# Attention backward: one block of E goes by way of GpSimd into the tile that a DMA transposes, and E lies in a ring of eleven steps

## The chip, the cores and the metric

The kernel runs on one core of a Trainium2 chip. The metric is the time of one execution on the device in microseconds (us); lower is better. The core has the matmul engine (PE; PEld is its loading of weights), VectorE (DVE), ScalarE (ACT), GpSimd (POOL) and SyncE (SP, which here only issues DMA transfers), and 16 DMA engines. PE, DVE, ACT, POOL and SP each run their own instructions in order and wait for one another by semaphores.

## The reference

Forward and gradients of `x + attention(LN(x)) * silu(MLP(LN(x)))`, for 2048 rows, width 512, 32 heads of 16 and a hidden width of 1792, all in bfloat16. Cut to the part that the change touches:

```python
qkv = (x @ wqkv).reshape(B, S, 3, H, Dh).transpose(2, 0, 3, 1, 4)
q, k, v = qkv[0], qkv[1], qkv[2]
scores = jnp.einsum("bhqd,bhkd->bhqk", q, k) * (Dh ** -0.5)
p = softmax(scores)
o = jnp.einsum("bhqk,bhkd->bhqd", p, v)
...
out, vjp = jax.vjp(f, A_x, A_wqkv, A_wo, B_w1, B_b1, B_w2, B_b2)
grads = vjp(grad_out)
```

With E = exp(scores - bound), D = dO V^T and G = D * E, the gradients of a head need E and G twice: with the keys on the partitions, as they are computed, and with the queries on the partitions, that is transposed.

## The kernel before

The attention loop (`attention_core`) takes two heads at a time (16 pairs) and 512 queries at a time (4 chunks): 64 blocks. Within a block it goes through the 2048 keys in 16 steps of 128 keys (`kb` 0 to 15), 1024 steps in all. The order of the work on every engine is written out by hand: the loop over `g` emits the parts of a step, and parts of earlier steps, in a fixed order, and each engine keeps it.

In step `g`, for both heads (`hj`), PE makes `s` (the scores of step g+1, L1115) and `d` (L1137) in PSUM; ACT writes the exponential of `s` into the tile `ets` (L1124), 8 blocks of 128 keys x 128 queries, numbered b = 2 * (query block) + head; DVE multiplies `d` by E into `gts` (L1153), one tile for two steps; PE adds up `X` (L1248, L1251, L1255), whose operands are E and G as they lie, and one step later transposes blocks of E through PSUM into `tT` (L1208, L1212). ACT, and DVE for a few blocks, copies these to the tile `ek` (L1224, L1231). `ek` holds 7 of the 8 blocks of E; the first block is left out of it in odd chunks of four steps, the last in even ones.

Two things are transposed by DMA, issued from SP (`emit_dmat`). All of G: after every second step one DMA transposes the 16 blocks of a `gts` tile into half a `gk` tile (L1170). And the one block of E that `ek` leaves out: a DMA transposes the four blocks of four steps, or eight blocks of two adjacent chunks at once, from `ets` into the tile `ekd` (L1180, L1184, L1186). It is issued in the steps with `kb % 8` of 4 and 6, so that a pair of chunks takes one issue or two, by where it lies in the ring. For this `ets` lies in three slots of four steps, `[128, 3, 4, 2, 4, 128]`: within a slot a block's four steps are neighbours. A slot's step is overwritten twelve steps later.

Twenty steps behind (`ZOFF`), `emit_z` (L1350) multiplies the transposed G (four steps of PE, one for each query block) and then the transposed E (four more) by small tiles `W` into `Z`, four matmuls a step; DVE adds `Z` to `acc` (L1362, L1364). GpSimd prepares `W` and the outputs of a block in two halves (`emit_fin`, L1311 to L1329), stores finished sums (`ob`, L1368 and L1371), and issues the loads of the next pair of heads, each behind a small copy `tick` (L1420), which waits for the step's products and so paces them. Tiles are reused in rings: `gts` 4, `gk` 6, `ekd` 3, `ek` 7.

Of the kernel before, what the change touches and what calls it, by code (L numbers as in the profile page):

```python
# [8 lines left out]
bf16 = mybir.dt.bfloat16  # L9
f32 = mybir.dt.float32  # L10
ACT = mybir.ActivationFunctionType
ALU = mybir.AluOpType
# [1038 lines left out]
def attention_core(ctx, ctx_r, tc, k, grads, Oall, dQall, dKVT_out, ident_f32, ident_bf, npairs=16, nqc=4):  # L1051
    nc = tc.nc
# [51 lines left out]
    def emit_s(g, hj):  # L1104
        a = a_unit(g)
        if a is None:
            return
        j, kb = a
        op = op_of(j)
        qc = blocks[j][1]  # L1110
        r = 32 * hj
        if hj == 0:
            cur["s"] = ps_s.tile([128, 2, 512], f32, name="s")
        s = cur["s"]
        nc.tensor.matmul(s[:, hj, :], lhsT=op["KVT"][r:r + 32, kb * 128:(kb + 1) * 128], rhs=op["QDT"][r:r + 32, qc * 512:(qc + 1) * 512],  # L1115
                         start=True, stop=True, tile_position=(r, 0))
        st_et[g] = ets[:, g // 4 % 3]

    def emit_exp(g):

        a = a_unit(g)
        if a is None:
            return
        nc.scalar.activation(out=st_et[g][:, :, :, a[1] % 4, :].rearrange("k b h q -> k h b q"),  # L1124
                             in_=cur["s"][:].rearrange("k h (b q) -> k h b q", b=4), func=ACT.Exp)

    def emit_d(g, hj):
# [13 lines left out]
    def emit_mult(g):  # L1141
        a = a_unit(g)
        if a is None:
            emit_xs(g - 1)
            emit_acc(g + ZOFF)
            return
        kb = a[1]
        if kb % 2 == 0:
            cur["gts"] = gtp.tile([128, 2, 2, 512], bf16, name="gts")
        gts = cur["gts"]  # L1150
        st_gt[g] = gts
        for hj in range(2):
            nc.vector.tensor_tensor(out=gts[:, kb % 2, hj, :].rearrange("k (b q) -> k b q", b=4),  # L1153
                                    in0=st_d.pop((g, hj))[:].rearrange("k (b q) -> k b q", b=4),
                                    in1=st_et[g][:, :, hj, kb % 4, :], op=ALU.mult)
            if hj == 0:
                emit_xs(g - 1)
                emit_acc(g + ZOFF)

    def emit_dmat(g):  # L1160
        a = a_unit(g)
        if a is None:
            return
        j, kb = a
        kc = kb // 4
        if kb % 4 == 1:
            blk[j]["Gk"][kc] = gbp.tile([128, 4, 2, 4, 128], bf16, name="gk")
        if kb % 2 == 1:
            gk = blk[j]["Gk"][kc][:, kb % 4 - 1:kb % 4 + 1]
            nc.sync.dma_start_transpose(out=gk.rearrange("q r h b k -> q (r h b) k"), in_=st_gt[g][:].rearrange("k a h q -> k (a h q)"))  # L1170


        sl = g // 4 % 3
        if kb % 8 == 4:
            ek = ekd.tile([128, 2, 4, 128], bf16, name="ekd")
            blk[j]["Ek"][(kc - 1, 3)] = ek[:, 0]
            blk[j]["Ek"][(kc, 3)] = ek[:, 1]
            blk[j]["ekd"] = ek
            if sl == 0:
                nc.sync.dma_start_transpose(out=ek[:, 0], in_=ets[:, 2, 3, 1].rearrange("k a q -> k (a q)"))  # L1180
        if kb % 8 == 6:
            ek = blk[j].pop("ekd")
            if sl == 0:
                nc.sync.dma_start_transpose(out=ek[:, 1], in_=ets[:, sl, 0, 0].rearrange("k a q -> k (a q)"))  # L1184
            else:
                nc.sync.dma_start_transpose(out=ek[:].rearrange("q c a k -> q (c a) k"),  # L1186
                                            in_=ets[:].rearrange("k s b h a q -> k (s b h) (a q)")[:, 8 * sl - 1:8 * sl + 1]
                                            .rearrange("k x q -> k (x q)"))

    OLDER = {4: (0, 0), 6: (0, 1), 7: (0, 2), 8: (5, 0), 12: (5, 1), 13: (5, 2)}  # L1190

# [6 lines left out]
    def emit_T(g):  # L1198
        a = a_unit(g)
        if a is None:  # L1200
            return
        kk = a[1] % 4
        et = st_et[g]
        t = ps_t.tile([128, 512], f32, name="tT")
        tb = t[:].bitcast(bf16).rearrange("q (i k) -> q i k", k=128)
        for i in range(cut(g), 7):
            b = i + a[1] // 4 % 2
            nc.tensor.transpose(tb[:, i - cut(g), :], et[:, b // 2, b % 2, kk, :], ident_bf[:])  # L1208
        if older(g):
            kk2, i = older(g)  # L1210
            b = i + kk2 // 4 % 2
            nc.tensor.transpose(tb[:, 7, :], st_et[g // 16 * 16 + kk2][:, b // 2, b % 2, kk2 % 4, :], ident_bf[:])  # L1212
# [20 lines left out]
    def emit_x(g, part):  # L1233
        a = a_unit(g)
        if a is None:
            return
        j, kb = a
        if part == "e" and kb == 0:
            blk[j]["X"] = ps_x.tile([128, 512], f32, name="X", tag="X")
        X = blk[j]["X"]  # L1240
        NATt = op_of(j)["NAT"]
        et = st_et[g]
        for c in range(4):
            half, hj = c // 2, c % 2
            r = 32 * c
            ev = et[:, half::2, hj, kb % 4, :]
            if part == "e":
                nc.tensor.matmul(X[r:r + 32, 0:256], lhsT=NATt[:, kb, hj, 1:33], rhs=ev,  # L1248
                                 start=(kb == 0), stop=False, skip_group_check=True, tile_position=(0, r))
            elif part == "l":  # L1250
                nc.tensor.matmul(X[r:r + 32, 256:512], lhsT=Lc[:], rhs=ev,  # L1251
                                 start=False, stop=False, skip_group_check=True, tile_position=(0, r))
            else:
                gv = st_gt[g][:, kb % 2, hj, :].rearrange("k (b q) -> k b q", b=4)[:, half::2, :]
                nc.tensor.matmul(X[r:r + 17, 256:512], lhsT=NATt[:, kb, hj, 0:17], rhs=gv,  # L1255
                                 start=False, stop=(kb == 15), skip_group_check=True, tile_position=(0, r))

# [74 lines left out]
    def emit_z(g):  # L1332
        u = z_unit(g)
        if u is None:
            return
        j, kp, qb, part = u
        if part == 0 and qb == 0:
            blk[j]["Z"] = ps_z.tile([128, 512], f32, name="Z", tag="z")
        Z = blk[j]["Z"]
        for par in range(2):  # L1340
            kc = 2 * kp + par
            for hj in range(2):
                r = 64 * par + 32 * hj
# [6 lines left out]
                nc.tensor.matmul(Z[r:r + 32, :], lhsT=WT[j % 2][1 - part][:, qb, hj, :], rhs=mv,  # L1350
                                 start=(part == 0 and qb == 0), stop=(part == 1 and qb == 3), tile_position=(0, r))

    def emit_acc(g):
        u = z_unit(g)
        if u is None or u[2] != 3 or u[3] != 1:
            return
        j, kp = u[0], u[1]
        p, qc = blocks[j]
        Z = blk[j]["Z"]
        av = acc[:, kp, :]  # L1360
        if qc == 0:
            nc.vector.tensor_copy(out=av, in_=Z[:])  # L1362
        else:
            nc.vector.tensor_tensor(out=av, in0=Z[:], in1=av, op=ALU.add)  # L1364
        if qc == nqc - 1:
            ob = (outp.tile([128, 512], bf16, name="ob") if kp == 0 or j < NB - 1 else
                  xsp.tile([128, 512], bf16, name="ob", tag="xs"))
            nc.gpsimd.tensor_copy(out=ob[:], in_=av)  # L1368
# [11 lines left out]
    for g in range(NSTEP - ZOFF):  # L1380
# [36 lines left out]
        for it in [x for x in late if x[0] <= g]:  # L1417
            late.remove(it)

            nc.gpsimd.tensor_copy(out=tick[:], in_=st_gt[g][0:1, kb % 2, 1, 510:512])  # L1420
            it[1]()
        if g >= NSTEP:
            grads.tail_mid(g - NSTEP)
# [120 lines left out]
```

## Time and profile before

| | us |
|---|---|
| median of three runs | 2192.32 |
| lowest and highest | 2185.16 and 2199.84 |
| the profiled execution | 2194.69 |
| its span | 2193.0 |

The attention loop fills the span from about 220 to 1870 us; what lies ahead of it (norms, projections, the MLP) and behind it (weight gradients) is not touched by the change. Over the whole span PE is busy for 98%, DVE for 86%, ACT for 81% and POOL for 27%; the granted clock of PE is full or nearly so in all slices. The page's matmuls overlap in the engine, so busy PE time is a sign of its order being full, not of peak rate. Groups of instructions are told by their line, engine and tiles (`gts<-d,ets` writes `gts` and reads `d` and `ets`); after a bar stand busy us, mean ns of one, and the engine's idle us before them with what ended it. For DMAs "landing" is the time from the issue to the completion.

### The profile page before, as it was taken

The numbers are of one execution on the slowest core, as the hardware profiler recorded it, in microseconds if no ns is written. First come the engines' busy times: TensorE is split into PE (matmuls) and PEld (weight loads), VectorE is DVE, ScalarE is ACT, GpSimd is POOL, SyncE is SP. The second block draws the span as 40 slices with busy tenths as digits, with TensorE's granted clock in tenths as the row PEclk, the third lists the DMA queues.
The fourth block names the chain that finished last, engine by engine and source line by source line (L and its number), as shares of the span: only waits on it lengthen the run. The fifth ranks groups of instructions, "written<-read, shape, count | busy, mean of one in ns | idle before, by whom it ended". The sixth has DMA issues, their size and how long they took to land.

```text
span 2193.0 us, 73789 instructions
## 1 busy us (share of the span) xinstructions
PE 2138.7 (98%) x30610; PEld 1173.8 (54%) x30659; DVE 1895.6 (86%) x3523; ACT 1782.5 (81%) x2481; POOL 596.8 (27%) x1373
## 2 busy tenths in 40 slices
PE   6999999999999999999999999999999999899999
PEld 3444555555555555555555555555555555444444
DVE  6677899999999999998999999999998998788647
ACT  5764899999999999998999999999998998675224
POOL 4275212232222222221313222222222222511003
PEclk9999999999999999999999999999999999999999
DMA  7786999999999999999999999999999999999975
GB/s 237 245 277 202 205 197 199 204 200 201 204 197 201 205 195 203 199 198 194 204 196 203 205 197 202 201 203 201 201 205 190 198 210 193 312 256 242 239 212 178
DMA packets 1422031, 461.11 MB, mean 210 GB/s; under 512 B 1334590, under 2 KB 1405886, under 8 KB 1421696
## 3 DMA queue, kind: packets, MB, share of 16 engines
q1 hardware_dynamic: 1407392, 425.46, 102.9%
q0 software_dynamic: 12720, 29.37, 5.1%
q8 instruction: 240, 3.93, 0.8%
q10 hardware_dynamic: 1584, 1.57, 0.2%
q14 instruction: 95, 0.78, 0.1%
HBM read 62.79 MB, written 64.75 MB: 58 GB/s over the span
## 4 chain that ended last, share of the span: by engine, by line
PE 89%; DMA 5%; DVE 3%; ACT 2%; issue 1%; SPq 1%; POOL 0%; DVEq 0%; ACTq 0%; POOLq 0%
PE tT L1208 21%; PE Z L1350 15%; PE d L1137 15%; PE X L1255 5%; PE X L1248 5%; PE X L1251 5%; PE s L1115 3%; DMA ekd<-ets 2%; PE ps_dy L909 2%; PE ps_dw L983 2%; PE ps_dw L742 2%; PE ps_h L352 2%; PE ps_m L367 2%; PE ps_dh L875 1%; PE ps_dxa L1027 1%; PE tT L1282 1%
## 5 line engine op out<-in xcount | busy, mean ns | idle before, releaser
L1153 DVE TENSOR_TENSOR gts<-d,ets 128x512 bf16<-128x512 f32 x2048 | 1302.1, 682 | 32.0 <-PE d L1137 13.7
L1124 ACT ACTIVATE ets<-s 128x1024 bf16<-128x1024 f32 x1024 | 1051.1, 1026 | 30.4 <-DMA ekd<-ets 10.3
L1224 ACT COPY ek<-tT 128x448 f32<-128x448 f32 (+1 forms) x1024 | 524.7, 512 | 114.9 <-PE tT L1208 33.2
L1208 PE MATMUL tT<-ident_bf,ets 128*128 128x128 bf16 x6790 | 558.4, 221 | 0.0
L1208 PEld LDWEIGHTS <-ets 128*128 128x128 bf16 x6790 | 382.8, 98 | 212.7 <-issue 199.7
L1137 PE MATMUL d<-QDT,KVT 32*128 32x512 bf16 x2048 | 478.4, 385 | 0.2 <-DVE gts L1153 0.2
L1115 PE MATMUL s<-QDT,KVT 32*128 32x512 bf16 x2048 | 401.9, 380 | 10.5 <-ACT ets L1124 10.4
L1248 PE MATMUL X<-ets,NAT 128*32 128x256 bf16 x4096 | 290.4, 273 | 0.0
L1251 PE MATMUL X<-ets,Lc 128*32 128x256 bf16 x4096 | 290.3, 273 | 0.0
L1255 PE MATMUL X<-gts,NAT 128*17 128x256 bf16 x4096 | 286.7, 273 | 0.0
L1350 PEld LDWEIGHTS <-W 128*32 128x32 bf16 x4096 | 105.7, 93 | 239.8 <-issue 236.9
L1420 POOL COPY tick<-gts 1x2 bf16<-1x2 bf16 x205 | 35.8, 174 | 728.6 <-DVE gts L1153 728.6
L1137 PEld LDWEIGHTS <-KVT 32*128 32x128 bf16 x2048 | 151.7, 90 | 114.5 <-issue 21.8
L1350 PE MATMUL Z<-gk,W 128*32 128x512 bf16 x2048 | 204.0, 390 | 1.4 <-DVE acc L1364 1.0
L1350 PE MATMUL Z<-ek,W 128*32 128x512 bf16 x1792 | 203.5, 389 | 0.0
L1251 PEld LDWEIGHTS <-Lc 128*32 128x32 bf16 x4096 | 109.9, 97 | 108.4 <-issue 0.5
L1231 DVE COPY ek<-tT 128x64 f32<-128x64 f32 x378 | 84.9, 225 | 90.9 <-ACT ek L1224 76.8
L1115 PEld LDWEIGHTS <-KVT 32*128 32x128 bf16 x2048 | 145.7, 91 | 25.5 <-issue 20.0
L1311 POOL TENSOR_TENSOR W<-NATQq,rL 128x128 bf16<-128x128 bf16 x64 | 25.5, 398 | 384.3 <-DVE rL L1310 328.7
L1255 PEld LDWEIGHTS <-NAT 128*17 128x17 bf16 x4096 | 112.9, 91 | 11.8 <-issue 3.1
L1248 PEld LDWEIGHTS <-NAT 128*32 128x32 bf16 x4096 | 109.5, 96 | 4.8 <-issue 4.7
L1350 PE MATMUL Z<-ekd,W 128*32 128x512 bf16 x256 | 99.6, 389 | 0.0
(252 smaller groups left out, 2467.2 us busy)
## 6 DMA issues: line engine op xcount, KB each, us to landing
gk<-gts SPq DMA_TRANSPOSE x512, 5.4
H1T_s<-h1r SPq DMA_DIRECT2D x28, 256.0 KB, 4.1
HGT_s<-hgT SPq DMA_DIRECT2D x8, 896.0 KB, 4.4
DH_s<-stg SPq DMA_DIRECT2D x12, 512.0 KB, 3.3
hch<-DH_s SPq DMA_DIRECT2D x12, 512.0 KB, 5.1
gp<-H1T_s SPq DMA_DIRECT2D x9, 512.0 KB, 7.1
out_dram<-ob_w POOLq DMA_DIRECT2D x36, 128.0 KB, 4.5
NAT_s<-NS SPq DMA_DIRECT2D x4, 1056.0 KB, 6.3
```

The costliest lines, as they stand in the source:

```text
L352: nc.tensor.matmul(ps[:], lhsT=w1_sb[:, ic, fc * 128:(fc + 1) * 128], rhs=yT[:, ic, g * 512:(g + 1) * 512], start=(ic == 0), stop=(ic == I ...
L1115: nc.tensor.matmul(s[:, hj, :], lhsT=op["KVT"][r:r + 32, kb * 128:(kb + 1) * 128], rhs=op["QDT"][r:r + 32, qc * 512:(qc + 1) * 512], start ...
L1124: nc.scalar.activation(out=st_et[g][:, :, :, a[1] % 4, :].rearrange("k b h q -> k h b q"), in_=cur["s"][:].rearrange("k h (b q) -> k h b q ...
L1137: nc.tensor.matmul(d[:], lhsT=op["KVT"][r:r + 32, kb * 128:(kb + 1) * 128], rhs=op["QDT"][r:r + 32, qc * 512:(qc + 1) * 512], start=True, ...
L1153: nc.vector.tensor_tensor(out=gts[:, kb % 2, hj, :].rearrange("k (b q) -> k b q", b=4), in0=st_d.pop((g, hj))[:].rearrange("k (b q) -> k b ...
L1208: nc.tensor.transpose(tb[:, i - cut(g), :], et[:, b // 2, b % 2, kk, :], ident_bf[:])
L1224: nc.scalar.copy(out=blk[j]["Ek"][kb // 4][:, kb % 4, c:7].rearrange("q i k -> q (i k)").bitcast(f32), in_=st_T[g][:, 0:(7 - c) * 64])
L1231: nc.vector.tensor_copy(out=blk[g // 16]["Ek"][kk // 4][:, kk % 4, i].bitcast(f32), in_=st_T[g][:, 448:512])
L1248: nc.tensor.matmul(X[r:r + 32, 0:256], lhsT=NATt[:, kb, hj, 1:33], rhs=ev, start=(kb == 0), stop=False, skip_group_check=True, tile_positi ...
L1251: nc.tensor.matmul(X[r:r + 32, 256:512], lhsT=Lc[:], rhs=ev, start=False, stop=False, skip_group_check=True, tile_position=(0, r))
L1255: nc.tensor.matmul(X[r:r + 17, 256:512], lhsT=NATt[:, kb, hj, 0:17], rhs=gv, start=False, stop=(kb == 15), skip_group_check=True, tile_pos ...
L1350: nc.tensor.matmul(Z[r:r + 32, :], lhsT=WT[j % 2][1 - part][:, qb, hj, :], rhs=mv, start=(part == 0 and qb == 0), stop=(part == 1 and qb = ...
```

## The change

The block of E that `ek` leaves out no longer goes from `ets` by a DMA of its own. In every step GpSimd copies it (128 x 128, bfloat16) into `gts`, which grows from 8 to 9 blocks a step, and the DMA that transposes two steps of `gts` moves 18 blocks, not 16, into a `gk` tile of 9 blocks a step. The tile `ekd` and its DMAs are gone; `emit_z` reads that block from `gk`. `ets` is then laid out step by step, in a ring of eleven. The query blocks of the second half of `Z` are taken in reversed order, so that the two blocks that come from `gk` are read in the first and the last of these four steps the other way round, and `emit_acc` and the closing matmul go with it.

```diff
-    ekd = sb("ekd", 3)
...
-    ets = etp.tile([128, 3, 4, 2, 4, 128], bf16, name="ets")
+    NE = 11
+    ets = etp.tile([128, NE, 4, 2, 128], bf16, name="ets")
...
     def z_unit(g):
         j = g // 16
         m = g % 8
-        return (j, (g % 16) // 8, m % 4, m // 4) if 0 <= j < NB else None
+        return (j, (g % 16) // 8, m if m < 4 else 7 - m, m // 4) if 0 <= j < NB else None
...
-        st_et[g] = ets[:, g // 4 % 3]
+        st_et[g] = ets[:, g % NE]
...
-        nc.scalar.activation(out=st_et[g][:, :, :, a[1] % 4, :].rearrange("k b h q -> k h b q"),
+        nc.scalar.activation(out=st_et[g].rearrange("k b h q -> k h b q"),
                              in_=cur["s"][:].rearrange("k h (b q) -> k h b q", b=4), func=ACT.Exp)
...
-            cur["gts"] = gtp.tile([128, 2, 2, 512], bf16, name="gts")
+            cur["gts"] = gtp.tile([128, 2, 9, 128], bf16, name="gts")
         gts = cur["gts"]
         st_gt[g] = gts
+        b = 7 * (1 - kb // 4 % 2)
+        nc.gpsimd.tensor_copy(out=gts[:, kb % 2, 8, :], in_=st_et[g][:, b // 2, b % 2, :])
         for hj in range(2):
-            nc.vector.tensor_tensor(out=gts[:, kb % 2, hj, :].rearrange("k (b q) -> k b q", b=4),
+            nc.vector.tensor_tensor(out=gts[:, kb % 2, 4 * hj:4 * hj + 4, :],
                                     in0=st_d.pop((g, hj))[:].rearrange("k (b q) -> k b q", b=4),
-                                    in1=st_et[g][:, :, hj, kb % 4, :], op=ALU.mult)
+                                    in1=st_et[g][:, :, hj, :], op=ALU.mult)
...
-            blk[j]["Gk"][kc] = gbp.tile([128, 4, 2, 4, 128], bf16, name="gk")
+            blk[j]["Gk"][kc] = gbp.tile([128, 4, 9, 128], bf16, name="gk")
         if kb % 2 == 1:
             gk = blk[j]["Gk"][kc][:, kb % 4 - 1:kb % 4 + 1]
-            nc.sync.dma_start_transpose(out=gk.rearrange("q r h b k -> q (r h b) k"), in_=st_gt[g][:].rearrange("k a h q -> k (a h q)"))
-
-
-        sl = g // 4 % 3
-        if kb % 8 == 4:
-            ek = ekd.tile([128, 2, 4, 128], bf16, name="ekd")
-            blk[j]["Ek"][(kc - 1, 3)] = ek[:, 0]
-            blk[j]["Ek"][(kc, 3)] = ek[:, 1]
-            blk[j]["ekd"] = ek
-            if sl == 0:
-                nc.sync.dma_start_transpose(out=ek[:, 0], in_=ets[:, 2, 3, 1].rearrange("k a q -> k (a q)"))
-        if kb % 8 == 6:
-            ek = blk[j].pop("ekd")
-            if sl == 0:
-                nc.sync.dma_start_transpose(out=ek[:, 1], in_=ets[:, sl, 0, 0].rearrange("k a q -> k (a q)"))
-            else:
-                nc.sync.dma_start_transpose(out=ek[:].rearrange("q c a k -> q (c a) k"),
-                                            in_=ets[:].rearrange("k s b h a q -> k (s b h) (a q)")[:, 8 * sl - 1:8 * sl + 1]
-                                            .rearrange("k x q -> k (x q)"))
+            nc.sync.dma_start_transpose(out=gk.rearrange("q r x k -> q (r x) k"), in_=st_gt[g][:].rearrange("k a x q -> k (a x q)"))
...
                 if part == 0:
-                    mv = blk[j]["Gk"][kc][:, :, hj, qb, :]
+                    mv = blk[j]["Gk"][kc][:, :, 4 * hj + qb, :]
                 elif 2 * qb + hj == 7 * (1 - par):
-                    mv = blk[j]["Ek"][(kc, 3)]
+                    mv = blk[j]["Gk"][kc][:, :, 8, :]
...
-                                 start=(part == 0 and qb == 0), stop=(part == 1 and qb == 3), tile_position=(0, r))
+                                 start=(part == 0 and qb == 0), stop=(part == 1 and qb == 0), tile_position=(0, r))
```

The readers of `ets` and `gts` in `emit_T`, `emit_x` and the `tick` change their indices alike; no instruction of PE, ACT or DVE is added or dropped.

More of the change, by code (lines that the diff above doesn't have):

```diff
@@ L1207, in emit_T @@
             b = i + a[1] // 4 % 2
-            nc.tensor.transpose(tb[:, i - cut(g), :], et[:, b // 2, b % 2, kk, :], ident_bf[:])
+            nc.tensor.transpose(tb[:, i - cut(g), :], et[:, b // 2, b % 2, :], ident_bf[:])
         if older(g):
@@ L1211, in emit_T @@
             b = i + kk2 // 4 % 2
-            nc.tensor.transpose(tb[:, 7, :], st_et[g // 16 * 16 + kk2][:, b // 2, b % 2, kk2 % 4, :], ident_bf[:])
+            nc.tensor.transpose(tb[:, 7, :], st_et[g // 16 * 16 + kk2][:, b // 2, b % 2, :], ident_bf[:])
         st_T[g] = t
@@ L1245, in emit_x @@
             r = 32 * c
-            ev = et[:, half::2, hj, kb % 4, :]
+            ev = et[:, half::2, hj, :]
             if part == "e":
@@ L1253, in emit_x @@
             else:
-                gv = st_gt[g][:, kb % 2, hj, :].rearrange("k (b q) -> k b q", b=4)[:, half::2, :]
+                gv = st_gt[g][:, kb % 2, 4 * hj + half:4 * hj + 4:2, :]
                 nc.tensor.matmul(X[r:r + 17, 256:512], lhsT=NATt[:, kb, hj, 0:17], rhs=gv,
@@ L1350, in emit_z @@
                 nc.tensor.matmul(Z[r:r + 32, :], lhsT=WT[j % 2][1 - part][:, qb, hj, :], rhs=mv,
-                                 start=(part == 0 and qb == 0), stop=(part == 1 and qb == 3), tile_position=(0, r))
+                                 start=(part == 0 and qb == 0), stop=(part == 1 and qb == 0), tile_position=(0, r))
     def emit_acc(g):
         u = z_unit(g)
-        if u is None or u[2] != 3 or u[3] != 1:
+        if u is None or u[2] != 0 or u[3] != 1:
             return
@@ L1418, in attention_core @@
             late.remove(it)
-            nc.gpsimd.tensor_copy(out=tick[:], in_=st_gt[g][0:1, kb % 2, 1, 510:512])
+            nc.gpsimd.tensor_copy(out=tick[:], in_=st_gt[g][0:1, kb % 2, 7, 126:128])
             it[1]()
```

## The prediction

> **What bounds the kernel now.** I read the page first, then one window over the attention loop, and then the list of waits.
>
> ```profile
> span 2193.0 us, 73789 instructions
> ...
> PE 89%; DMA 5%; DVE 3%; ACT 2%; issue 1%; SPq 1%; POOL 0%; DVEq 0%; ACTq 0%; POOLq 0%
> PE tT L1208 21%; PE Z L1350 15%; PE d L1137 15%; PE X L1255 5%; PE X L1248 5%; PE X L1251 5%; PE s L1115 3%; DMA ekd<-ets 2%; PE ps_dy L909 2%; PE ps_dw L983 2%; PE ps_dw L742 2%; PE ps_h L352 2%; PE ps_m L367 2%; PE ps_dh L875 1%; PE ps_dxa L1027 1%; PE tT L1282 1%
> ...
> L1153 DVE TENSOR_TENSOR gts<-d,ets 128x512 bf16<-128x512 f32 x2048 | 1302.1, 682 | 32.0 <-PE d L1137 13.7
> L1124 ACT ACTIVATE ets<-s 128x1024 bf16<-128x1024 f32 x1024 | 1051.1, 1026 | 30.4 <-DMA ekd<-ets 10.3
> ```
>
> ```profile
> 220.00:1870.00 1650.00, 1637.29 (x27939) 929.46 (x27938) 1513.88 (x2819) 1496.32 (x2054) 417.97 (x1151) 1.00 1.17 201
> ```
>
> The second fence is one row of busy time for the stretch from 220 to 1870 us; after its length come PE, PEld, DVE, ACT and POOL, then the granted clock, the DMA share and GB/s. The 1024 exponentials are the 1024 steps of the loop, so a step takes 1650 / 1024 = 1.61 us. In the stretch PE is idle for 1650 - 1637.3 = 12.7 us, DVE for 136 us (0.13 us a step), ACT for 154 us. PE sets the pace, with DVE and ACT close behind it, and the chain of waits says the same: 89% PE. A change that leaves the instructions of PE as they are, as this one does, can gain little more than those 12.7 us by taking waits away; it can lose much more if it makes PE, ACT or DVE wait.
>
> ```profile
> POOL tick L1420 <- DVE gts L1153: 728.6, 190, 6.7
> ...
> PE s L1115 <- ACT ets L1124: 10.4, 13, 1.9
> ...
> ACT ets L1124 <- DMA ekd<-ets: 10.3, 11, 2.1
> ...
> DVE gts L1153 <- DMA gk<-gts: 0.6, 1, 0.6
> ```
>
> These are waits in total us, times, and longest. One chain fills PE's idle time: the exponential waits for a DMA transpose that still reads the part of `ets` it must overwrite (10.3 us), and the next `s` on PE waits for that exponential (10.4 us). The other kind of transpose, `gk` from `gts`, has held the products up once. The longest of those stalls, on ACT and on the queue of SP:
>
> ```profile
> 1028.29 0.53 ACT L1224 COPY ek<-tT 128x448 f32<-128x448 f32 x1
> 1030.90 1.02 ACT L1124 ACTIVATE ets<-s 128x1024 bf16<-128x1024 f32 x1 [2.07 <-DMA ekd<-ets]
> 1031.82 0.53 ACT L1224 COPY ek<-tT 128x448 f32<-128x448 f32 x1
> 1032.45 1.02 ACT L1124 ACTIVATE ets<-s 128x1024 bf16<-128x1024 f32 x1
> 1034.24 0.53 ACT L1224 COPY ek<-tT 128x448 f32<-128x448 f32 x1 [0.77 <-PE tT L1208]
> ```
>
> ```profile
> 1013.60 12.62 SPq L1170 DMA_TRANSPOSE gk<-gts  x4
> 1026.31 1.26 SPq L1186 DMA_TRANSPOSE ekd<-ets  x1
> 1027.66 6.99 SPq L1170 DMA_TRANSPOSE gk<-gts  x3
> ```
>
> SP issued four `gk` transposes without a pause from 1013.60 to 1026.22, and the transpose of `ekd` had to stand behind them. The exponential then started 2.07 us late, and 0.77 us more followed on ACT two steps later. So the fault is the place of the `ekd` transpose in SP's queue, together with the short time before its source is overwritten.
>
> **Part by part: the transposes.**
>
> ```profile
> L1170 SPq DMA_TRANSPOSE gk<-gts x512: 1589/2282/4537, 227.0 to 1858.6; - x171
> ...
> DMA to landing us min/median/max: 3.7/5.4/8.6
> ```
>
> ```profile
> L1186 SPq DMA_TRANSPOSE ekd<-ets x85: 1260/1270/2438, 234.0 to 1843.8; - x85
> L1180 SPq DMA_TRANSPOSE ekd<-ets x43: 1207/1213/2227, 243.5 to 1853.1; - x43
> L1184 SPq DMA_TRANSPOSE ekd<-ets x43: 1207/1220/2551, 247.3 to 1857.3; - x43
> ...
> DMA to landing us min/median/max: 2.3/4.3/6.4
> ```
>
> Each row gives the issue on SP in ns, least, median and most. Removed: 85 x 1.27 + 43 x 1.213 + 43 x 1.22 = 213 us of SP. Now SP issues 512 x 2.282 + 213 = 1381 us in 1650 us, 84%. Added: each `gk` transpose grows from 16 to 18 blocks of 128x128. The blocks moved stay the same: 85 x 8 + 86 x 4 = 1024 leave and 512 x 2 = 1024 come. Least issues of 8 and 16 blocks differ by (1589 - 1260) / 8 = 41 ns a block, so 82 ns more each; in proportion to the medians it would be 2.282 x 18/16 = 2.57 us. SP then issues 1210 to 1314 us, 73 to 80%. I take the lower end for the sum, because the two least rows are unloaded ones, and keep the other for the range; on either SP gets freer. Least landings of 4 and 16 blocks, 2.3 and 3.7 us, give 0.12 us a block, so an 18-block one lands some 0.2 us later.
>
> Cover: the ring of `gts` has four tiles of two steps, so eight steps or 12.9 us from the first product of a pair to the first product that reuses its tile. The pair's last product ends one step and two products, 1.61 + 2 x 0.68 = 3.0 us, after its first begins. That leaves 9.9 us for queueing and landing; the longest landing now is 8.6 us. With 0.2 us more a few loaded pairs may run out: I take +1 us in all, from 0 to 5 (8 waits like the one of 0.6 us). What stands behind a late transpose on SP is only the next one, and the `Z` matmuls read `gk` 13 steps after its last pair, so nothing else feels it.
>
> **The removed wait.** Gain: at least the 10.3 us of ACT. At the quoted stall 2.07 us cost 2.84 with what followed, so at most 10.3 x 2.84 / 2.07 = 14.1; PE's idle time allows 12.7. I take 12.
>
> **The copies on GpSimd.**
>
> ```profile
> L1420 POOL COPY tick<-gts 1x2 bf16<-1x2 bf16 x205 | 35.8, 174 | 728.6 <-DVE gts L1153 728.6
> ...
> L1325 POOL TENSOR_TENSOR t<-xs,t 128x128 f32<-128x128 f32 x64 | 29.4, 459 | 5.0
> L1322 POOL TENSOR_TENSOR Oall<-xs,rL 128x128 bf16<-128x128 f32 x64 | 26.5, 414 | 14.7 <-DVE xs L1290 13.5
> L1324 POOL TENSOR_TENSOR t<-xs,ndl 128x128 f32<-128x128 f32 x64 | 25.9, 404 | 0.0
> L1329 POOL TENSOR_TENSOR dQall<-t,rL 128x128 bf16<-128x128 f32 x64 | 25.7, 402 | 5.3
> ...
> L1368 POOL CAST ob<-acc 128x512 bf16<-128x512 f32 x32 | 19.4, 607 | 42.3 <-DVE acc L1364 42.3
> ...
> L1327 POOL TENSOR_SCALAR rL<-rL 128x8 f32<-128x8 f32 x64 | 14.6, 228 | 0.0
> ```
>
> No copy of 128x128 stands in the trace. Between the 1x2 copy (174 ns) and the 128x512 cast (607 ns) it would take 174 + 126 x 433 / 510 = 281 ns; the bounds are 174 and the 402 ns of a two-input 128x128. So 1024 x 0.281 = 288 us (178 to 412) on a POOL that is busy for 418 of 1650 us: 43% after. In its order a copy stands behind the five operations of the final half, 0.414 + 0.404 + 0.459 + 0.228 + 0.402 = 1.9 us, behind a tick that waits for this step's products, or behind the cast of `ob`. Behind a late copy wait the transpose of its pair, up to about 1 us later than the products would let it go (within the range of the term above), and the exponential eleven steps on. The latter is issued ten steps later, some 16 us, against a delay of 2 to 3 us: nothing. PE's own last reader of an `ets` slot is the transpose that unit 13 makes of step 5, issued in loop step 14, one before the exponential that overwrites it; PE's order covers the eleventh slot where there were twelve. The `W` products find at most one copy in front, 0.28 us, and the late loads have four blocks of lead: nothing.
>
> **The added wait on ACT.** Each exponential now also waits for POOL.
>
> ```profile
> L1124 ACTq EVENT_SEMAPHORE  x1183: 17/358/1456, 219.8 to 1853.8; - x198
> ```
>
> Such a wait takes 17 ns when it is already met, and the median one, 358 ns, is the wait for `s` on PE under the running copy. Cost 0, because the extra one fits into those 358 ns; without that cover 1024 x 17 ns = 17 us.
>
> **The new layouts.** Same lengths of run, other strides.
>
> ```profile
> L1350 PE MATMUL Z<-gk,W x2048: 376/390/609, 253.7 to 1866.8; 128*32 128x512 bf16 x187
> L1350 PE MATMUL Z<-ek,W x1792: 379/390/392, 259.9 to 1867.7; 128*32 128x512 bf16 x200
> L1350 PE MATMUL Z<-ekd,W x256: 379/389/390, 260.0 to 1867.7; 128*32 128x512 bf16 x128
> ```
>
> Three strides (eight, seven and one block from row to row) read at the same 389 to 390 ns, so nine blocks cost nothing, and `ekd` within `gk` neither. The reversed order of the second half of `Z` frees a `gk` tile of the first chunk in loop step 24 and its next transpose is issued in step 25: PE's order again, no cost.
>
> **GpSimd against DVE.**
>
> ```profile
> L1153 DVE TENSOR_TENSOR gts<-d,ets x2048: 647/681/693, 221.4 to 1856.7; 128x512 bf16<-128x512 f32 x187
> ```
>
> All 2048 products lie between 647 and 693 ns although POOL works in a quarter of the stretch, so its work does not draw them out: cost 0, from 0 to the whole 0.281 us of a copy a step (second rival). The Trainium skill, in "Perfetto Trace Analysis", section "Optimizing Scalar/DVE Operations", warns that GpSimd and DVE share an SBUF read port, so that moving work between them might not help; in "SBUF — State Buffer", section "Who interferes with whom", it narrows this to DVE instructions with two SBUF inputs or in a two-port mode. The product has one input in PSUM, and the row above goes with the narrower rule.
>
> **Sum.** -12 + 1 = -11 us, against the profiled execution's 2194.7 (span 2193.0): 2183.7. That run lies 2.4 us above the median of 2192.3, so on the median it is 2181, -0.5%.
>
> **The rivals.** (A) The wait changes its name: the exponential waits for the POOL copy, or for the products that are then next late, instead of for `ekd`. For: ACT and DVE have little room. Against: ten steps of lead. Time: 2192. (B) Slower: the bigger transposes outrun the ring of `gts`. Its place is the first product of a pair, waiting for the landing of four pairs ago, and it decides from a landing plus queue of 9.9 us on. If an 18-block transpose goes as two, a second one as small as the 2.3 us landing adds to 5.4 and 8.6: 7.7 in the median, 10.9 at worst, before queueing. With one pair in eight waiting 1 us that is 64 us: 2192 + 64 - 11 = 2245. For: the DMA share of the window row is 1.17, and SP has run 12.62 us without a pause. Against: the issue grows by block, and SP loses 171 issues. (C) The copies hold DVE's port (the wider of the two rules makes this case, too). 0.281 us a step against 0.13 us of idle time: 0.15 x 1024 = 154 us, 2192 + 154 - 11 = 2335. Against it stands the row of 693 ns at most. (D) All the idle time ahead of the exponentials goes, 30.4 us by the page: 2162. Against: 20 of them lie in waits the change doesn't touch.
>
> **How the numbers follow.** Forecast 0.60, A 0.12, B 0.16, C 0.06, D 0.06. The forecast's own range is 2171 to 2204: below, 2192.3 - 14.1 for the wait - 7 for the spread of the three runs about their median; above, 2192.3 - 10.3 + 5 for the ring + 17 for ACT's extra wait. The limit of 1%, about what a measurement of this kernel tells from no change, lies at 2170 and 2214. Faster by more: D and a sliver of the forecast, 0.07; slower: B and C, 0.22; within: 0.71. The range of eight in ten leaves out D below 2170 and C with half of B above 2235.
>
> **What would show it.** Right: no wait of the exponentials on a DMA; the POOL copies near 280 ns and POOL near 43%; SP issues of least about 1.67 us, none of `ekd`; PE idle in the attention stretch under 4 us; products still 681 ns. Wrong: products waiting for `gk` tens of times (B); products over 700 ns (C); exponentials waiting for POOL (A); a landing of 18 blocks above 7 us in the median.

## The result, and the profile after

| | before, us | after, us |
|---|---|---|
| median of six runs each | 2194.71 | 2179.59 |
| lowest and highest | 2185.16 and 2199.84 | 2176.10 and 2181.20 |
| the profiled execution | 2194.69 | 2180.46 |
| its span | 2193.0 | 2178.8 |

The ratio is 0.9934 with a 95% interval of 0.9913 to 0.9954: the change takes about 14.5 us off, between 10 and 19. It also narrows the runs: before they lie within 14.7 us, after within 5.1.

The page of the changed kernel, its span, the chain of waits and the two groups shown of before (after the bar: busy us, mean ns, and idle us ahead with what ended it):

```profile
span 2178.8 us, 74934 instructions
...
PE 94%; DVE 2%; DMA 1%; ACT 1%; POOL 0%; issue 0%; SPq 0%; DVEq 0%; ACTq 0%; POOLq 0%
...
L1155 DVE TENSOR_TENSOR gts<-d,ets 128x512 bf16<-128x512 f32 x2048 | 1302.2, 682 | 18.2 <-PE d L1137 3.9
L1124 ACT ACTIVATE ets<-s 128x1024 bf16<-128x1024 f32 x1024 | 1051.6, 1027 | 15.2 <-PE d L1137 3.9
...
L1153 POOL COPY gts<-ets 128x128 bf16<-128x128 bf16 x1024 | 281.6, 297 | 387.5 <-ACT ets L1124 382.7
```

The DMA share of the chain went from 5% to 1% and PE's from 89% to 94%. ACT's idle time ahead of the exponentials halved, from 30.4 to 15.2 us. The instructions of DVE and ACT kept their lengths.

The busy time over the loop, from 220 us to its earlier end at 1856 us (length; PE, PEld, DVE, ACT, POOL; clock, DMA share, GB/s):

```profile
220.00:1856.00 1636.00, 1632.56 (x27961) 928.69 (x27957) 1517.99 (x2819) 1496.59 (x2056) 692.78 (x2178) 1.00 1.14 203
```

PE is idle for 3.4 us where it was for 12.7, and busy for 1632.6 us where it was for 1637.3. The two stretches were chosen to end with the loop and differ by 14 us, so 9.3 us of it left as idle time and 4.7 us as busy time, with the same instructions. Most of the 4.7 us goes with the clock. In the kernel before, PE's two longest gaps were waits of `s` for a held-up exponential: 1.80 us up to 1031.97 us, and 1.86 us up to 1683.01. Shortly after each of them the granted clock (third number from the end) stood at half for 3.4 us. The rows of the kernel before show the end of the first gap, then seven transposes within the slow stretch and seven after it; the second fence has the busy time of both slow stretches:

```profile
1031.97 0.39 PE L1115 MATMUL s<-QDT,KVT 32*128 32x512 bf16 x2 [1.80 <-ACT ets L1124]
...
1033.28 0.93 PE L1208 MATMUL tT<-ident_bf,ets 128*128 128x128 bf16 x7
...
1037.44 0.56 PE L1208 MATMUL tT<-ident_bf,ets 128*128 128x128 bf16 x7
```

```profile
1032.60:1036.00 3.40, 3.40 (x45) 1.56 (x38) 1.80 (x4) 2.43 (x3) 0.00 (x0) 0.50 1.12 245
1684.50:1687.90 3.40, 3.40 (x37) 1.59 (x40) 1.29 (x2) 2.09 (x4) 0.00 (x0) 0.50 1.07 228
```

Seven such transposes took 0.93 us there and 0.56 us afterwards. Two stretches of 3.4 us at half the clock are worth some 3.4 us of PE, an estimate from these rows; the other 1.3 us are not explained. In the changed kernel the clock is full from 227 to 1906 us. This is one execution of each kernel; how many such stretches the others had is not known.

The waits of the changed kernel that answer to those of before (from 215 to 1860 us), in total us, times and longest:

```profile
POOL gts L1153 <- ACT ets L1124: 382.7, 323, 1.6
POOL tick L1404 <- DVE gts L1155: 313.5, 190, 2.2
...
POOL gts L1153 <- DMA gk<-gts: 3.3, 2, 2.2
...
PE s L1115 <- ACT ets L1124: 2.4, 2, 1.3
```

No exponential waits for a DMA any more, and PE waits for exponentials for 2.4 us instead of 10.4. What waits for the `gk` transposes is now the copy on GpSimd, twice. GpSimd's 383 us behind the exponentials are idle time of an engine with room.

### The profile page after: what moved, and what is told of

Same layout as the page of the kernel before. It is cut to its first block, busy times and chain, and to the rows that moved or that the text cites. A ratio compares the mean times of both kernels' runs of the same rounds, so it can differ in the third digit from the quotient of the medians.

```text
span 2178.8 us, 74934 instructions
## 1 busy us (share of the span) xinstructions
PE 2133.0 (98%) x30659; PEld 1170.6 (54%) x30659; DVE 1898.0 (87%) x3523; ACT 1782.2 (82%) x2481; POOL 870.6 (40%) x2397
## 3 DMA queue, kind: packets, MB, share of 16 engines
q10 hardware_dynamic: 1584, 1.57, 0.2%
## 4 chain that ended last, share of the span: by engine, by line
PE 94%; DVE 2%; DMA 1%; ACT 1%; POOL 0%; issue 0%; SPq 0%; DVEq 0%; ACTq 0%; POOLq 0%
PE tT L1192 22%; PE Z L1334 15%; PE d L1137 15%; PE X L1239 6%; PE X L1232 5%; PE X L1235 5%; PE s L1115 3%; PE ps_dy L909 2%; PE ps_dw L742 2%; PE ps_dw L983 2%; PE ps_h L352 2%; PE ps_m L367 2%; PE ps_dh L875 2%; PE tT L1266 1%; PE ps_dxa L1027 1%; PE ps_dwkv L827 1%
## 5 line engine op out<-in xcount | busy, mean ns | idle before, releaser
L1124 ACT ACTIVATE ets<-s 128x1024 bf16<-128x1024 f32 x1024 | 1051.6, 1027 | 15.2 <-PE d L1137 3.9
L1137 PE MATMUL d<-QDT,KVT 32*128 32x512 bf16 x2048 | 469.4, 384 | 0.0
L1153 POOL COPY gts<-ets 128x128 bf16<-128x128 bf16 x1024 | 281.6, 297 | 387.5 <-ACT ets L1124 382.7
L1334 PE MATMUL Z<-gk,W 128*32 128x512 bf16 x2304 | 302.9, 389 | 1.4 <-DVE acc L1348 1.3
L1137 PEld LDWEIGHTS <-KVT 32*128 32x128 bf16 x2048 | 148.5, 91 | 114.3 <-issue 21.5
L1115 PEld LDWEIGHTS <-KVT 32*128 32x128 bf16 x2048 | 142.7, 91 | 12.3 <-issue 6.4
```

Source lines behind the costliest of these rows:

```text
L1124: nc.scalar.activation(out=st_et[g].rearrange("k b h q -> k h b q"), in_=cur["s"][:].rearrange("k h (b q) -> k h b q", b=4), func=ACT.Exp)
L1137: nc.tensor.matmul(d[:], lhsT=op["KVT"][r:r + 32, kb * 128:(kb + 1) * 128], rhs=op["QDT"][r:r + 32, qc * 512:(qc + 1) * 512], start=True, ...
L1153: nc.gpsimd.tensor_copy(out=gts[:, kb % 2, 8, :], in_=st_et[g][:, b // 2, b % 2, :])
```

## The experiments

Each kernel was timed against the kernel before on the same chip, but not all on one chip, so differences between two of them are taken from their ratios, times 2195 us. Rows of the profile are of one execution each; for `two_blocks` and `even_two` it was the slowest of all their runs, so their rows may show more waiting than the median run had. SP's share of the loop is the sum of all its issues of transposes in the loop, added up over the trace, over the time from the start of the first exponential to the start of the last. The changed kernel has a ratio of 0.9934.

| run | median, us | ratio, 95% interval |
|---|---|---|
| own_as_before | 2185.70 | 0.9932, 0.9907 to 0.9957 |
| no_move | 2179.28 | 0.9926, 0.9906 to 0.9946 |
| z_order | 2178.16 | 0.9923, 0.9903 to 0.9943 |
| dummy_issue | 2265.31 | 1.0322, 1.0297 to 1.0347 |
| dummy_no_move | 2180.07 | 0.9931, 0.9906 to 0.9956 |
| own_transpose | 2231.27 | 1.0165, 1.0144 to 1.0186 |
| two_blocks | 2235.30 | 1.0166, 1.0122 to 1.0210 |
| even_two | 2187.53 | 0.9954, 0.9931 to 0.9977 |
| copy_twice | 2248.23 | 1.0213, 1.0190 to 1.0235 |
| copy_const | 2179.68 | 0.9918, 0.9886 to 0.9950 |
| copy_dve | 2221.39 | 1.0094, 1.0068 to 1.0119 |

### Is it the freed wait, or the shorter queue on SP?

Two readings of the gain stand against each other below. T: it comes from freeing `ets`, so that no exponential waits for a DMA. R: it comes from the shorter queue on SP.

**own_transpose**: the copy stays, the merging is undone, one transpose of four blocks every four steps.

```diff
+    ecp = sb("ecp", 2)
...
+        if kb % 4 == 0:
+            cur["ec"] = ecp.tile([128, 4, 128], bf16, name="ec")
+        nc.gpsimd.tensor_copy(out=cur["ec"][:, kb % 4, :], in_=st_et[g][:, b // 2, b % 2, :])
...
+            nc.sync.dma_start_transpose(out=ek, in_=cur["ec"][:].rearrange("k a q -> k (a q)"))
...
```

> GpSimd copies the block of E into a tile of its own, and SP transposes it by a DMA of its own, four blocks every four steps (256 issues, more than the 171 of the kernel before), so the merging is undone and the copy stays. Theory T (the gain is that no exponential waits for a DMA that reads ets): time stays at 2176 to 2187, no wait of an exponential on a DMA, PE idle in the loop under 5 us. Rival R (the gain is the shorter queue on SP, 213 us of issues less): SP issues some 512 x 2.28 + 256 x 1.21 = 1477 us, more than before the change, so the gain is gone: 2192 to 2200.

Measured 2231.27, outside what either theory said. No exponential waited for a DMA, as T has it; but a new wait came in. The rows of the tile `ekd` and the waits of this run:

```profile
L1181 SPq DMA_TRANSPOSE ekd<-ec x256: 1188/1219/2483, 231.7 to 1893.5; - x128
```

```profile
POOL ec L1157 <- DMA ekd<-ec: 534.4, 193, 6.8
...
DVE gts L1159 <- DMA gk<-gts: 33.5, 50, 2.4
...
PE d L1139 <- DVE gts L1159: 22.7, 40, 1.6
```

The products wait 50 times for a `gk` transpose of four pairs ago, and PE's `d` for the products: this is rival B of the prediction, brought about by too many issues. The rows account for 23 of the 51 us by which the run lies over the changed kernel; the rest is not assigned, and the 534 us that GpSimd waits ahead of its copies may have a part in it. The issues on SP take 1590 us of a loop of 1667 (95%), against 1475 of 1634 (90%) in the kernel before and 1412 of 1619 (87%) in the changed one. So this run does not decide between T and R.

**own_as_before**: the same, with the 171 transposes of the kernel before in their old places, but for the 128 of them that came in the steps with `kb % 8` of 6 and now come one step later, so that SP's load is the old one, too. To make room for the new tile the finished sums are cast in place.

```diff
...
+    ecs = ecp.tile([128, 3, 4, 128], bf16, name="ecs")
...
+        nc.gpsimd.tensor_copy(out=ecs[:, g // 4 % 3, kb % 4, :], in_=st_et[g][:, b // 2, b % 2, :])
...
+        if kb % 8 == 4:
...
+            if sl == 0:
+                nc.sync.dma_start_transpose(out=ek[:, 0], in_=ecs[:, 2].rearrange("k a q -> k (a q)"))
+        if kb % 8 == 7:
...
+                nc.sync.dma_start_transpose(out=ek[:].rearrange("q c a k -> q (c a) k"),
+                                            in_=ecs[:, sl - 1:sl + 1].rearrange("k s a q -> k (s a q)"))
...
```

> The changed kernel with the merging undone and the transposes of that block as in the kernel before: 171 of four and eight blocks, in the same places of SP's queue (the later one a step later), read from a tile of three slots into which GpSimd copies; gk transposes of 16 blocks again. SP issues as long as before the change, some 512 x 2.28 + 213 = 1381 us. T (the exponentials' wait on a DMA is the whole gain, the copy gives it): no such wait, PE idle in the loop under 5 us, 2176 to 2184. R (the merging is the gain, by the shorter queue on SP): 2190 to 2200, with products or copies waiting for DMA instead.

Measured 0.9932, the ratio of the changed kernel: 2185.70 us, a little over the range given by T, on a chip where the kernel before took 2199.72. The waits and the loop's busy row of this run:

```profile
POOL ecs L1156 <- DMA ekd<-ecs: 131.0, 56, 5.7
```

```profile
220.00:1840.00 1620.00, 1615.16 (x27706) 920.55 (x27707) 1499.35 (x2795) 1486.02 (x2041) 680.47 (x2155) 1.00 1.18 202
```

The wait for the small transposes is still there, and is even longer, 131 us in 56 waits, but it is GpSimd that waits, ahead of its copy into the tile. PE is idle for 4.8 us. SP's issues take 1484 of 1623 us, no less than before the change. So T holds and R falls: the gain comes from freeing `ets` by a copy, and the merging by itself gives nothing that can be measured here (the two intervals, 0.9907 to 0.9957 and 0.9913 to 0.9954, overlap).

**no_move** takes the transport of the block away altogether: one block of E is left out of the sums, and `Z` reads a block of G in its place.

```diff
...
-        nc.gpsimd.tensor_copy(out=gts[:, kb % 2, 8, :], in_=st_et[g][:, b // 2, b % 2, :])
...
-                    mv = blk[j]["Gk"][kc][:, :, 8, :]
+                    mv = blk[j]["Gk"][kc][:, :, 7, :]
```

> The changed kernel without any transport of that block of E: no copy, transposes of 16 blocks, and Z reads a block of G in its place, so one block of E is left out of the sums. It shows what the move costs in its new form. T: the copy and the two more blocks are hidden, so 2172 to 2180, at most 7 us under the changed kernel. R: SP gets another 512 x 0.24 = 125 us back, and time falls in proportion to the gain seen for 213 us, by about 9 us: 2166 to 2172.

2179.28 us: the copies and the two more blocks of each transpose cost nothing that can be measured in the changed kernel, although SP's issues take only 71% of the loop here (1150 of 1616 us). Between 71% and the 91% of `own_as_before` SP's load made no measurable difference.

### Where the queue does count

**dummy_issue** and **dummy_no_move**: 171 idle transposes in the old places, in the changed kernel and in `no_move`.

```diff
+    dmy = outp.tile([128, 48], bf16, name="dmy")
...
+        if kb % 8 == 6 or (kb % 8 == 4 and g // 4 % 3 == 0):
+            nc.sync.dma_start_transpose(out=dmy[:, 0:16], in_=ident_bf[0:16, :])
```

> The changed kernel with idle transposes of a constant (16 rows) issued on SP in the very steps in which the kernel before issued its transposes of ekd, 171 in all; ets is not read by them. T: 2178 to 2184, since nothing of the exponentials' hangs on SP. R: SP has its 200 us again and most of the gain is given back, 2189 to 2196.

> The kernel without the transport of that block of E (left out of the sums, 16-block transposes) with the 171 idle transposes of the earlier run on SP. SP then issues some 512 x 2.11 + 171 x 1.18 = 1283 us, 78% of the loop, against 91% in the earlier run that lost 86 us. If the loss came from SP and the DMA engines being too full for the ring of gts: nothing here, 2176 to 2184, waits on gk under 5 us. If a small transpose between two large ones always costs: 2230 to 2270.

The first one lost 85 us against the changed kernel, far more than either theory allowed. The waits of `dummy_issue` from 215 to 1900 us:

```profile
POOL gts L1153 <- DMA gk<-gts: 176.2, 116, 4.3
...
DVE gts L1155 <- DMA gk<-gts: 54.9, 68, 2.6
...
PE d L1137 <- DVE gts L1155: 41.9, 55, 2.2
```

In the kernel without the transport the same 171 transposes cost nothing measurable (ratios of 0.9931 and 0.9926). So a small transpose between large ones is not dear as such; the loss goes with the sum. With 1633 of 1704 us on SP (96%) transposes fall behind until the ring of `gts` has no free tile, the products wait, and PE waits for them. With some 85% (1372 of 1621) products wait on `gk` for 3.0 us in all. In between stands own_as_before, at 91% and without loss. PE's waits of 41.9 us are half of the 85; the other half stands in the rows as longer busy time and is not assigned.

The trace also shows where the transposes fall behind. From the last product of a pair to the start of its transpose's issue the median is 0.7 us in the changed kernel and 3.7 in `dummy_issue` (3.5 in `own_transpose`, 3.4 in `two_blocks`, 2.2 in `even_two`). From the end of the issue to the landing, where the trace has it, the median is 2.7 us in the changed kernel and in `dummy_issue` alike, and between 230 and 1840 us their DMA shares are 1.14 and 1.09. So the delay arises ahead of the issue, in SP's order, and not behind it.

**z_order**: the old order of the query blocks in the second half of `Z`.

```diff
-        return (j, (g % 16) // 8, m if m < 4 else 7 - m, m // 4) if 0 <= j < NB else None
+        return (j, (g % 16) // 8, m % 4, m // 4) if 0 <= j < NB else None
...
```

> The changed kernel with the query blocks of the second half of Z in the old order, so that the first chunk's gk tile is read until loop step 27 and the transpose issued in step 25 must wait for that, about 1.9 us longer than for its products. Expected by T: the delay eats into the slack of the gts ring once in four pairs and is mostly covered, 2180 to 2200, with more waits of products or copies on gk. If the reversed order does nothing: 2176 to 2182 and no such waits.

2178.16 us, and no wait of products or copies on `gk` among the waits listed: the reversed order makes no difference. The delay of 1.9 us that was expected did not show at all: none of SP's waits in this run names a matmul of `Z`, and the transpose in question starts 0.75 us after its products in the median, as in the changed kernel (0.74).

### The copy: how much, and on which engine

**copy_twice** makes every copy twice.

```diff
-        nc.gpsimd.tensor_copy(out=gts[:, kb % 2, 8, :], in_=st_et[g][:, b // 2, b % 2, :])
+        for _ in range(2):
+            nc.gpsimd.tensor_copy(out=gts[:, kb % 2, 8, :], in_=st_et[g][:, b // 2, b % 2, :])
```

> The changed kernel with every copy on GpSimd made twice, 1024 x 0.297 = 304 us more of POOL, which is then busy for some 61% of the loop. If the copies are hidden and hold nothing of DVE's: products at 681 ns, 2176 to 2186. If GpSimd's reads of SBUF hold the products up: 0.3 us a step against some 0.12 us idle on DVE, up to 2360, and products above 700 ns or with gaps ahead of them. If the late copies hold up the transposes: waits on gk as in the run with idle transposes, 2190 or more.

It lost 61 us against the changed kernel (the expectation below counts 68, from the medians), and by none of the three ways: no wait on `gk` stands in its list, and the products kept their 680 ns. What changed shows on ACT. The row of the products and the timeline of ACT in `copy_twice`:

```profile
L1156 DVE TENSOR_TENSOR gts<-d,ets x2048: 677/680/693, 219.0 to 1909.0; 128x512 bf16<-128x512 f32 x187
```

```profile
1000.67 1.02 ACT L1124 ACTIVATE ets<-s 128x1024 bf16<-128x1024 f32 x1
1001.75 0.53 ACT L1209 COPY ek<-tT 128x448 f32<-128x448 f32 x1
1002.31 1.02 ACT L1124 ACTIVATE ets<-s 128x1024 bf16<-128x1024 f32 x1
1003.33 0.53 ACT L1209 COPY ek<-tT 128x448 f32<-128x448 f32 x1
1003.95 1.02 ACT L1124 ACTIVATE ets<-s 128x1024 bf16<-128x1024 f32 x1
1004.97 0.53 ACT L1209 COPY ek<-tT 128x448 f32<-128x448 f32 x1
1005.59 1.02 ACT L1124 ACTIVATE ets<-s 128x1024 bf16<-128x1024 f32 x1
```

And in the changed kernel:

```profile
1000.31 1.03 ACT L1124 ACTIVATE ets<-s 128x1024 bf16<-128x1024 f32 x1
1001.44 0.53 ACT L1208 COPY ek<-tT 128x448 f32<-128x448 f32 x1
1001.87 1.03 ACT L1124 ACTIVATE ets<-s 128x1024 bf16<-128x1024 f32 x1
1003.03 0.53 ACT L1208 COPY ek<-tT 128x448 f32<-128x448 f32 x1
1003.46 1.03 ACT L1124 ACTIVATE ets<-s 128x1024 bf16<-128x1024 f32 x1
1004.53 0.53 ACT L1208 COPY ek<-tT 128x448 f32<-128x448 f32 x1
1005.01 1.02 ACT L1124 ACTIVATE ets<-s 128x1024 bf16<-128x1024 f32 x1
```

From exponential to exponential it is exactly 1.64 us in the first, and 1.57 on the mean in the second (4.70 / 3); over the whole loop the medians are 1.640 and 1.571 us. From the start of ACT's copy to the next exponential it is 0.56 to 0.62 us against 0.43 to 0.48: in the changed kernel the exponential mostly starts before the copy of 0.53 us has ended, with the second copy only after it. ACT's separate wait instructions ahead of the exponentials, of `copy_twice` and of the changed kernel (count, least, median and most ns):

```profile
L1124 ACTq EVENT_SEMAPHORE  x2028: 17/38/38, 217.5 to 1906.5; - x185
```

```profile
L1124 ACTq EVENT_SEMAPHORE  x1015: 38/361/657, 218.2 to 1837.0; - x170
```

In the changed kernel an exponential waits for three semaphores: DVE's and PE's in one wait instruction, GpSimd's on the exponential itself. The second copy brings a fourth, ACT's own, and with it a second wait instruction; the wait for PE's scores is then the first of them, and the others stand behind it, on the path from the scores to the exponential. From the end of the first wait instruction to the start of the exponential the median is 121 ns instead of 56, which is nearly the 69 ns that a step got longer. That this path sets the loop is inferred from that agreement.

**copy_const** tells the wait from the load of GpSimd: two copies a step, the first of a constant.

```diff
+        nc.gpsimd.tensor_copy(out=gts[:, kb % 2, 8, :], in_=ident_bf[:])
         nc.gpsimd.tensor_copy(out=gts[:, kb % 2, 8, :], in_=st_et[g][:, b // 2, b % 2, :])
```

> The run with every copy made twice lost 68 us, and its exponentials wait for four semaphores instead of three, the later ones behind the wait for the scores. Here GpSimd also makes two copies a step into the same place, first of a constant and then of E, so that its load is that of the run before, but the exponentials wait for three semaphores, as in the changed kernel. If the fourth wait cost the 68 us: 2178 to 2188, loop steps at the changed kernel's length. If the load of GpSimd did: 2240 to 2255 again.

2179.68 us. The rows of the wait instructions and of the loop in this run:

```profile
L1124 ACTq EVENT_SEMAPHORE  x1015: 38/360/657, 219.4 to 1838.2; - x170
```

```profile
220.00:1840.00 1620.00, 1617.65 (x27779) 920.01 (x27782) 1508.52 (x2802) 1490.82 (x2046) 961.45 (x3183) 1.00 1.15 203
```

GpSimd is busy for 59% of the stretch and it costs nothing, with steps of 1.572 us in the median; so the loss of the run before was the fourth wait, 61 us / 1024 = 0.06 us a step. (The first copy here does not wait for the exponential, as it did there; no other difference is left between the two runs.)

**copy_dve**: `nc.vector.tensor_copy` in place of `nc.gpsimd.tensor_copy`.

> The changed kernel with the copy on VectorE. DVE idles 0.12 us a step; the nearest copy of its own, 128x64 f32 out of PSUM, takes 225 ns, so DVE becomes the bound by some 0.05 to 0.15 us a step: 2230 to 2330. If a copy within SBUF costs DVE under 0.1 us, it is hidden: 2178 to 2190.

2221.39 us, 35 more than the changed kernel by the ratios and between the two expectations. The copy on DVE (least, median, most):

```profile
L1153 DVE COPY gts<-ets x1024: 144/183/2177, 219.4 to 1879.9; 128x128 bf16<-128x128 bf16 x171
```

It is shorter than the 225 ns that it was priced by, and shorter than GpSimd's 297, but DVE had only 0.12 us a step to give; 35 us / 1024 = 0.03 us a step came on top. That DVE is the bound there fits but is not shown: between 230 and 1870 us it is still idle for 67 of 1640 us.

### One block further

**two_blocks** lets the DMA move 20 blocks a pair and PE transpose six a step instead of seven; **even_two** does so in every other chunk.

```diff
-        nc.gpsimd.tensor_copy(out=gts[:, kb % 2, 8, :], in_=st_et[g][:, b // 2, b % 2, :])
+        nc.gpsimd.tensor_copy(out=gts[:, kb % 2, 8:10, :], in_=st_et[g][:, b, :, :])
...
-        for i in range(cut(g), 7):
-            b = i + a[1] // 4 % 2
+        for i in range(cut(g), 6):
+            b = i + 2 * (a[1] // 4 % 2)
```

> The change carried one block further: GpSimd copies two blocks of E, the DMA moves 20, PE transposes six blocks a step instead of seven, ACT copies 384 columns instead of 448, and the older blocks that DVE copies fall from six to four a block; the sums to be stored are cast in place to make room. If the ring of gts holds: PE saves 1024 x 56 ns = 57 us, 2118 to 2140. If the transposes become the bound (SP some 512 x 2.77 = 1418 us in 1580, 90%, near the 91% of the run with idle transposes, which lost 85 us): products and copies wait for gk tens of times, 2165 to 2230.

> Two blocks of E by the DMA in the even chunks, one in the odd ones: 19 blocks a transpose on average, between the changed kernel's 18 (no waits on gk) and 20 (waits of some 220 us, 2235). SP: half at 2.53, half at 2.92 us, 1395 us, 87% of 1610. PE saves half of 57 us. If the ring holds: 2148 to 2160, faster than both kernels. If it is already over the edge: 2180 to 2220, with waits of products and copies on gk of 20 to 100 us.

Measured 2235.30 and 2187.53 us: the second branch both times. The transposes of `two_blocks`, and who waited for them:

```profile
L1172 SPq DMA_TRANSPOSE gk<-gts x512: 2362/2923/6442, 228.8 to 1914.4; - x171
...
who waited for it (us, times):
  POOL gts L1153: 167.3, 115
  DVE gts L1155: 69.2, 81
...
DMA to landing us min/median/max: 4.1/6.0/10.0
```

SP issues for 1627 of 1689 us (96%) there and for 1557 of 1631 (95%) in `even_two`, whose copies waited for `gk` for 56 us. What PE should have saved, 57 us by the expectation, is more than eaten by the ring of `gts` in `two_blocks`. The clock has a part in it: in the profiled execution it stood at half for 41 us of the loop, which by the reckoning above is worth some 20 us. `even_two` is under the kernel before (0.9954), and its runs reach from 2177.59 to 2199.83 us; it does not beat the changed kernel. No version that was run is measurably faster than that one.

## Why the prediction was right

The forecast was 2181 us; 2179.59 was measured. As a change it was -11 us, and -14.5 was measured, by 10 to 19. That the two times lie only 1.4 us apart is partly luck: the sum ended on the median of three runs of the kernel before, 2192.32, and with six runs that median is 2194.71. By its steps:

- **The removed wait.** Forecast -12 us between 10.3 and 14.1; the ratio gives 14.5. The cause was the one named: own_as_before keeps the number of the issues and, to within a step, their place on SP, and gains as much, by the copy that frees `ets`. The bound that was read from PE's idle time, 12.7 us, was too tight: stalls also cost busy time. The two longest were each followed by 3.4 us at half the clock, some 3.4 us together, which the sum left out.
- **The transposes.** Here the sizes were off, in the two bounds that were to cover them. An issue of 18 blocks was taken at 82 ns over one of 16, from the step between 8 and 16 blocks. The row of the changed kernel:

```profile
L1172 SPq DMA_TRANSPOSE gk<-gts x512: 1827/2527/4732, 228.0 to 1840.7; - x171
...
DMA to landing us min/median/max: 3.9/5.6/7.7
```

The least issue rose from 1589 to 1827, by 119 ns a block instead of 41, so the sign of about 1.67 us did not come; the median of 2527 is near the other bound, 2.57 us. And SP's share, reckoned with medians, came out at 84% before and 73 to 80% after. The issues of the trace add up to 90 and 87%: the long ones weigh more than the median shows. The landing, 0.2 us later, and the ring's cost, 3.3 us of waits on GpSimd and none on DVE, came as forecast.
- **The copies.** 297 ns, where 281 was worked out; GpSimd busy for 693 of 1636 us, 42%, where 43% was. Hidden, as forecast: copy_const carries twice the load.
- **The added wait on ACT.** Cost nothing, but the reason given was wrong. No wait instruction was added: GpSimd's semaphore took the place of ACT's own, and with the DMA's gone the count fell from 1183 to 1015. The prediction took 17 ns each as the worst; copy_twice shows what one more costs where it stands behind the wait for the scores, 0.06 us a step. Had the change needed it, the gain would have turned into a loss.
- **Layouts and the order of Z.** Nothing, as forecast: z_order.
- **GpSimd against DVE.** The products of the changed kernel:

```profile
L1155 DVE TENSOR_TENSOR gts<-d,ets x2048: 676/681/693, 219.8 to 1839.9; 128x512 bf16<-128x512 f32 x187
```

693 ns at most, as before, with 1024 copies beside them. In `copy_const`, with GpSimd at 59%, they took 694 ns at most. This goes with the narrower rule of the Trainium skill ("SBUF — State Buffer", section "Who interferes with whom"), as the product has one input in PSUM. The wider warning of the Trainium skill ("Perfetto Trace Analysis", section "Optimizing Scalar/DVE Operations"), that moving work between GpSimd and DVE might not help, is not borne out for this product. Rival C, priced at 2335 us, did not happen.
- **The rivals.** A and D did not happen. B did not happen in this kernel, but it was near: its place and its mechanism were right, and it comes as soon as SP's issues fill about 95% of the loop, at 51 to 85 us over the changed kernel (own_transpose, two_blocks and dummy_issue; the rival had 64). `even_two`, also at 95%, lies only some 4 us over it, what PE saved taken off. That the loss begins between 91% and 95% is read from these runs. The transposes fall behind in SP's queue and not between issue and landing; what sets the length of an issue under load is not known.

## What to carry to other kernels

A transfer that reads a ring buffer keeps its slot until the transfer has come through its queue; a copy by an idle engine into a tile of the transfer's own moves that wait to an engine that has time for it. Before more work is put on a DMA queue, add up its issues rather than multiply a median: at 87 to 91% of the loop this one cost nothing, and three of the four runs at 95 to 96% lost more than the whole change had gained. And a wait of PE can cost more than its own length, where the clock drops after it. Look, too, at how many semaphores the pacing instruction waits for: a reader on one more engine can be free or cost a wait instruction in every step.

## What was not expected of the hardware

The issue of a transpose on SP is not linear in its blocks: least durations were 1111 ns for 16 rows of one block, 1188 for four blocks, 1260 for eight, 1589 for 16, 1827 for 18 and 2362 for 20. From 16 blocks on each one more costs 0.12 to 0.27 us, about three to six times the 41 ns between eight and 16. (The other runs with 18 blocks have a least issue of 1808 to 1892 ns. The row for 20 comes from a queue that was hardly ever empty, so an unloaded issue may be shorter.)

The wait for a fourth semaphore made ACT's step 1.64 us instead of 1.57. Of the 65 ns that were added between the first wait and the exponential 38 are the second wait instruction itself, and the rest lies between the instructions.

In the loops of all runs, their first and last 10 us left out, the clock fell to half only at the end of a gap of PE of 1.1 to 2.5 us or up to 2.1 us after it, for 3.4 or 6.8 us at a time: twice in the kernel before, three times in `dummy_issue`, once in `even_two`, ten times in `two_blocks`. Not every such gap did it: `dummy_issue` has 15 gaps of 1.0 us and more. What decides is not shown here.
